# Weight scales from a norm instead of a maximum, unscaled relu values, and a second split of the weights

## The chip, the cores and the metric

The kernel runs on one core of a Trainium2 chip. The metric is the device time of one execution in microseconds; before the change the median of three runs is 1149.46 us.

## The reference

Attention with a mask that comes from clusters is followed by two expert layers. All of it is computed in float32:

```python
def _attn_ref(q, k, v, centroids):            # q, k, v (2, 8, 768, 64), centroids (8, 16, 64)
    q_n = q / (np.linalg.norm(q, axis=-1, keepdims=True) + 1e-06)      # k_n, c_n alike
    q_assign = np.argmax(np.einsum('bhsd,hcd->bhsc', q_n, c_n), axis=-1)
    mask = q_assign[:, :, :, None] == k_assign[:, :, None, :]
    scores = np.where(mask, scale * np.matmul(q, k.transpose(0, 1, 3, 2)), -1e9)
    attn = softmax(scores)
    return np.matmul(attn, v)

def _moe_ref(x, w_in, w_out):                 # x (1536, 512), w_in (512, 2048), w_out (2048, 512)
    h = x @ w_in
    return (h * np.clip(h + 3.0, 0.0, 6.0) / 6.0) @ w_out

def _moe2_ref(x, domain_probs, w1, w2):       # w1 (4, 512, 1024), w2 (4, 1024, 512)
    p = domain_probs / (domain_probs.sum(-1, keepdims=True) + 1e-09)
    for e in range(4):
        out += p[:, e:e + 1] * (np.maximum(x @ w1[e], 0.0) @ w2[e])
```

## The kernel before

Every float32 product of the expert layers is made of three float16 matmuls: each operand is split into a high half (its float16 rounding) and a low half (the rest), and high x high, high x low and low x high are summed in PSUM (mm3, lines 966 to 968). For float16 to hold the values, each weight matrix of 512 x 512 is first multiplied by a scale. The scale comes from the matrix's largest absolute value, and what it takes away is given back in later factors (kt, wu, pq). GSC and XSC are fixed powers of two in that bookkeeping.

The work falls into stages: attention of batch 0 (Attn.turned); Moe1, the first layer, of batch 0; Moe2, the second layer, of batch 0 together with attention of batch 1 (Attn.block); Moe1 of batch 1; Moe2 of batch 1. A batch has 768 tokens in two blocks of 384. Moe1 runs over four chunks of 512 hidden columns, Moe2 over eight; a chunk has two weight matrices ("i" and "o", or "1" and "2"), each of four tiles of 128 x 512. In batch 1 all chunks but the first use a scheme with seven instead of eight block products (class Wino, PSUM pool ps_w), which needs sums of weight blocks (sums_w).

Three helpers prepare weights. conv_w (line 936) takes the first layer's matrices, which arrive as float64 words, and builds float32 tiles from the bits (lines 947 to 955: an Abs on ScalarE, four VectorE instructions a tile, the first of which also accumulates the maximum). load_w (898) takes Moe2's matrices for batch 0: four raw tiles loaded (raw_w, 888), an absolute maximum of each on VectorE (903). Both then call allmax (510) to get one number for all 128 partitions. Without a PSUM pool it writes the column of maxima to DRAM (516), reads it back spread to all partitions (518) and takes a maximum over it (519). Then split_w (866) scales the tiles (GpSimd, for "2" ScalarE), rounds the high half (ScalarE, 874), subtracts the low half (GpSimd, 875) and writes the pair to DRAM as hl_* (886). again_w (908) reads these pairs; Moe1 reads them in both batches, Moe2 in batch 1. sums_w (915) loads the raw tiles of "1" once more for its sums.

Moe2.post (1199) turns a result of the first product into the operand of the second: Relu from PSUM with scale GSC into a float32 tile t (1202, ScalarE), the high half h[:, 0] from t (1203, ScalarE), and the low half h[:, 1] from t and h[:, 0] (1204, VectorE or GpSimd). A product's PSUM tile comes from p_m, three banks, in batch 0, and from ps_w, five banks, in the Wino chunks.

The order of instructions on every engine is fixed when the program is built: class Order takes all tasks with a priority (the table PAR and offsets in the code set it), places each on its engine at the time its own cost table says is earliest, lower priority numbers first, and emits them in that order. Each engine, SyncE's DMA queue too, then works its list strictly in order. Buffers come from pools in groups; the PSUM group of batch 0's attention (g_pa, with the pool ps_ma) closes before the group with p_m opens.

## Time and profile before

| | us |
|---|---|
| runs | 1149.46 median (1140.43 to 1151.48, three runs) |
| profiled execution | 1153.14 |
| its span, first to last instruction | 1151.4 |
| TensorE busy, instructions | 985.5 (86%), 5669 matmuls |
| VectorE busy | 792.5 (69%) |
| ScalarE busy | 566.8 (49%) |
| GpSimd busy | 398.9 (35%) |
| DMA, all 16 engines | 150.89 MB, mean 131 GB/s |
| mean granted TensorE clock | 0.938 of full speed |

PE is TensorE, PEld its weight loads, DVE VectorE, ACT ScalarE, POOL GpSimd, SP SyncE; a q behind a name is that engine's sequencer, so SPq is where SyncE's DMA instructions are issued and wait. In the table a busy share is a mean over stages with different limits, so the rows further down go by stretches. An instruction is named by its line in the listing above and by "out<-in" in the program's names.

### The profile page before, as it was taken

The page shows a single profiled execution, that of the slowest core. Times are in us where ns is not written, and L with a number is a line of the kernel's source. Part 1 is how long each engine was busy: PE and PEld are TensorE (multiplying, and loading weights), DVE is VectorE, ACT ScalarE, POOL GpSimd, SP SyncE. Part 2 cuts the span into 40 slices and gives each one's busy share as a digit, 9 for nine tenths or more (in the row PEclk, how much of TensorE's full clock was granted, in tenths as well). Part 3 has the DMA queues.
Part 4 walks back from the last instruction along what each step waited for, and adds up shares of the span by engine and source line. Part 5 has one row for each costly group of instructions (what it writes and reads, how often), then busy time and mean ns, then how long its engine had stood idle before and what let it go on. Part 6 is the DMA issues. An engine that isn't in the chain of part 4 may idle for free.

```text
span 1151.4 us, 16297 instructions
## 1 busy us (share of the span) xinstructions
PE 985.5 (86%) x5669; PEld 574.1 (50%) x5669; DVE 792.5 (69%) x1636; ACT 566.8 (49%) x1070; POOL 398.9 (35%) x376
## 2 busy tenths in 40 slices
...
GB/s 299 100 84 118 136 184 138 258 213 104 118 126 117 140 79 196 153 142 130 145 159 163 144 172 106 191 161 151 112 117 110 65 67 86 106 109 74 73 38 55
DMA packets 145778, 150.89 MB, mean 131 GB/s; under 512 B 86880, under 2 KB 89952, under 8 KB 145696
## 3 DMA queue, kind: packets, MB, share of 16 engines
...
## 4 chain that ended last, share of the span: by engine, by line
PE 44%; DVE 19%; DMA 18%; issue 9%; POOL 6%; ACT 3%; SPq 1%; POOLq 0%; ACTq 0%; DVEq 0%
DMA pt<-p 6%; PE psm L966 5%; PE psm L968 5%; PE psm L967 5%; PE psg L966 4%; PE psg L967 4%; PE psg L968 4%; PE psw L1043 4%; PE psw L1045 4%; PE psw L1044 4%; DVE ut L830 3%; DMA wraw<-in_w 3%; DVE p L854 2%; POOL w L875 2%; DMA bc<-mx 1%
## 5 line engine op out<-in xcount | busy, mean ns | idle before, releaser
L968 PE MATMUL psm<-w,h 128*128 128x512 f16 x384 | 149.6, 390 | 17.6 <-DVE h L1204 12.7
L966 PE MATMUL psm<-w,h 128*128 128x512 f16 x384 | 150.0, 391 | 0.0
L967 PE MATMUL psm<-w,h 128*128 128x512 f16 x384 | 149.3, 389 | 0.0
L1204 POOL TENSOR_TENSOR h<-t,h 128x384 f16<-128x384 f32 x32 | 29.2, 919 | 330.6 <-ACT h L1203 310.7
L831 ACT ACTIVATE e<-pss,ut 128x768 f32<-128x768 f32 x96 | 86.2, 899 | 90.5 <-DVE ut L830 54.1
L967 PEld LDWEIGHTS <-w 128*128 128x128 f16 x704 | 70.5, 100 | 66.0 <-issue 25.0
L966 PE MATMUL psm<-x2h,w 128*128 128x384 f16 x288 | 98.4, 342 | 1.9 <-ACT x2h L1161 1.4
L1204 DVE TENSOR_TENSOR h<-t,h 128x384 f16<-128x384 f32 x96 | 68.5, 714 | 45.6 <-ACT h L1203 45.4
L967 PE MATMUL psm<-x2l,w 128*128 128x384 f16 x288 | 97.9, 340 | 0.5 <-DVE x2l L1163 0.5
L966 PEld LDWEIGHTS <-w 128*128 128x128 f16 x704 | 70.5, 100 | 54.1 <-issue 12.3
L968 PE MATMUL psm<-x2h,w 128*128 128x384 f16 x288 | 97.4, 338 | 0.0
L968 PEld LDWEIGHTS <-w 128*128 128x128 f16 x704 | 70.7, 100 | 51.4 <-issue 8.1
L830 DVE TENSOR_REDUCE ut<-pss 128x1 f32<-128x768 f32 x96 | 90.3, 946 | 8.7 <-PE pss L825 8.3
L1229 DVE SCALAR_TENSOR_TENSOR oa<-psm,pq,oa 128x512 f32<-128x512 f32 x84 | 62.6, 745 | 46.5 <-PE psm L968 45.9
L875 POOL TENSOR_TENSOR w<-wraw,w 128x512 f16<-128x512 f32 x64 | 81.3, 1284 | 32.6 <-ACT w L874 27.6
L966 PE MATMUL psg<-g,w 128*128 128x384 f16 x256 | 84.1, 329 | 3.9 <-DVE t L1110 3.4
L967 PE MATMUL psg<-g,w 128*128 128x384 f16 x256 | 84.2, 329 | 0.9 <-POOL g L1112 0.6
L823 PE MATMUL pss<-ka,qa 128*128 128x384 f32 x192 | 64.1, 417 | 23.5 <-ACT e L831 21.4
L968 PE MATMUL psg<-g,w 128*128 128x384 f16 x256 | 84.1, 329 | 0.0
L739 PE MATMUL pst<-ident,e 128*128 128x128 f32 x288 | 49.3, 309 | 33.6 <-ACT pt L746 16.1
L903 DVE TENSOR_REDUCE am<-wraw 128x1 f32<-128x512 f32 x64 | 42.7, 677 | 50.3 <-DMA wraw<-in_w 50.2
L968 PEld LDWEIGHTS <-h 128*128 128x128 f16 x384 | 38.4, 100 | 69.2 <-DVE h L1204 22.6
(197 smaller groups left out, 2352.9 us busy)
## 6 DMA issues: line engine op xcount, KB each, us to landing
wraw<-in_w SPq DMA_DIRECT2D x92, 256.0 KB, 4.5
hl<-w SPq DMA_DIRECT2D x64, 256.0 KB, 4.3
w<-hl SPq DMA_DIRECT2D x64, 256.0 KB, 3.1
...
w<-hl_i SPq DMA_DIRECT2D x32, 256.0 KB, 3.6
w<-hl_o SPq DMA_DIRECT2D x32, 256.0 KB, 3.8
...
```

The source lines that it names most:

```text
L739: nc.tensor.transpose(ps[:, t // 3, t % 3 * 128:t % 3 * 128 + 128], e[:, x:x + 128], ident.t)
L823: nc.tensor.matmul(ps[:, f, 0:HS], qa[:, qs], ka[:, f * HS:f * HS + HS], start=True, stop=False)
L830: dve(S, p, lambda: nc.vector.tensor_reduce(out=nb(), in_=ps[:, :, 0:HS], axis=AX.XY, op=ALU.max, negate=True), [ps], [(tb, n)])
L831: act(S, p, lambda: nc.scalar.activation(out=e.t.rearrange("p (a b) -> p a b", a=2), in_=ps[:, :, 0:HS], func=AF.Exp, bias=nb(), scale=1.0 ...
L875: pool(512, p, lambda w=w, raw=raw: nc.gpsimd.tensor_tensor(out=w[:, 1], in0=raw.t, in1=w[:, 0], op=ALU.subtract), [raw, (w, 0)], [(w, 1)])
L966: nc.tensor.matmul(o_, ah, bh, start=i == 0, stop=False)
L967: nc.tensor.matmul(o_, ah, bl, start=False, stop=False)
L968: nc.tensor.matmul(o_, al, bh, start=False, stop=i == 3)
L1043: nc.tensor.matmul(o_, ah, bh, start=k == 0, stop=False)
L1044: nc.tensor.matmul(o_, ah, bl, start=False, stop=False)
L1204: low = lambda e: e.tensor_tensor(out=h[:, 1], in0=t.t, in1=h[:, 0], op=ALU.subtract)
L1229: dve(512, p, lambda: nc.vector.scalar_tensor_tensor(out=oa[:, t], in0=ps.t, scalar=q, in1=oa[:, t], op0=ALU.mult, op1=ALU.add), [ps, qk], ...
```

## The change

The scale of a weight matrix comes from its Frobenius norm. load_w squares each raw tile on ScalarE with an accumulated sum; conv_w squares the accumulated maxima of its tiles instead of reducing them. The new helper norm adds over partitions with a matmul against a tile of ones, sums four columns and clamps on VectorE, takes the square root as a power on GpSimd and the reciprocal on VectorE. The DRAM way of allmax is gone; its PSUM way stays for activations. conv_w is given a PSUM pool: ps_ma for the first two matrices, p_m for the other six.

Moe2.post rounds the relu straight from PSUM to the high half and gets the low half from PSUM too, always on VectorE; the tile t and the factor GSC are gone. Moe2's pairs are no longer written to DRAM in batch 0: in batch 1 the raw tiles are loaded and split again (split_w), and sums_w uses these tiles. The numbers of PAR are others, and Order adds 1.5 us (spm) to what a DMA waits for when it plans.

```diff
-XSC = 8192.0
-GSC = 2.0 ** -20
+XSC = 8.0
+WSC = 256.0
...
-    ta=43.32610950668564,
-    tu=2.3993615910477435,
+    ta=44.84286963635529,
+    tu=2.588310665078212,
...
-    mx=30.0,
-    sp=14.0,
-    spc=4.0,
+    mx=31.25809700336469,
+    sp=10.020641134361943,
+    spc=4.775375938290964,
...
-    slow=1.1868260418282515,
+    slow=1.0810926227241242,
...
-    cv0=90.0,
-    cvd=22.0,
+    cv0=130.0,
+    cvd=16.891660848559347,
+    cva=2,
...
-                                s = max(s, o.end)
+                                s = max(s, o.end + (PAR["spm"] if e == "SP" else 0.0))
...
-    ones = fixed([1, 128], F32, "ones")
+    ones = fixed([128, 128], F32, "ones")
...
+    def norm(am, cols, p, pp):
+
+        inv, ki, sc, ks = cols
+        ps = Buf(pp, [128, 4], F32, "psn")
+        pe(0.25, p, lambda: nc.tensor.matmul(ps.t, ones.t, am[:, 0:4], start=True, stop=True), [am], [ps])
+        dve(4, p, lambda: nc.vector.tensor_reduce(out=inv, in_=ps.t, axis=AX.X, op=ALU.add), [ps], [ki])
+        dve(1, p, lambda: nc.vector.tensor_scalar(out=inv, in0=inv, scalar1=1e-30, scalar2=1.0 / WSC ** 2, op0=ALU.max, op1=ALU.mult), [], [ki])
+        pool(2, p, lambda: nc.gpsimd.tensor_tensor(out=inv, in0=inv, in1=half[:, 0:1], op=ALU.pow), [], [ki], ns=172.0)
         dve(1, p, lambda: nc.vector.reciprocal(out=sc, in_=inv), [ki], [ks])
...
             if dst is None:
                 wt.setdefault(key, []).append(w)
+                continue
...
-            dma(262e3, p + (0 if dst else 4), lambda w=w, scr=scr: nc.sync.dma_start(out=scr.t, in_=w.t), [w], [scr])
+            dma(262e3, p, lambda w=w, scr=scr: nc.sync.dma_start(out=scr.t, in_=w.t), [w], [scr])
...
-            dve(512, p - PAR["mx"], lambda k=k, raw=raw: nc.vector.tensor_reduce(
-                out=am[:, k:k + 1], in_=raw.t, axis=AX.X, op=ALU.max, apply_absolute_value=True), [raw], [(am, k)])
-        allmax(am, 4, inv, ki, 1.0 / XSC, sc, ks, p - PAR["mx"])
+            act(512, p - PAR["mx"], lambda k=k, raw=raw: nc.scalar.activation(
+                out=mxj.t, in_=raw.t, func=AF.Square, accum_out=am[:, k:k + 1]), [raw], [(am, k)], acc=True)
+        norm(am, wcol(*key[1:]), p - PAR["mx"], p_m)
...
-                if key[1] == "1":
-                    act(512, p, lambda x=x: nc.scalar.activation(out=x.t, in_=x.t, func=AF.Copy, scale=sc), [ks], [x], ap=True)
...
-        allmax(am, 4, inv, ki, 1.0 / XSC, sc, ks, p, bits=True)
+        dve(4, p, lambda: nc.vector.tensor_tensor(out=am[:, 0:4], in0=am[:, 0:4], in1=am[:, 0:4], op=ALU.mult), [], [am])
+        norm(am, wcol(*key[1:]), p, pp)
...
-                again_w(key, p)
+                raws = raw_w(lambda k: src[:, k], p - 4)
+                split_w(key, raws, p)
                 if n == "1" and self.wino(c):
-                    sums_w(key, lambda k: src[:, k], p)
+                    sums_w(key, raws, p)
...
-            t = Buf(p_t[self.b], [128, MB], F32, "t")
             h = Buf(p_gw if self.wino(c) and blk else p_g, [128, 2, MB], F16, "h")
-            act(MB, p, lambda: nc.scalar.activation(out=t.t, in_=out(), func=AF.Relu, scale=GSC), [ps], [t], ps=True)
-            act(MB, p, lambda: nc.scalar.activation(out=h[:, 0], in_=t.t, func=AF.Copy), [t], [(h, 0)])
-            low = lambda e: e.tensor_tensor(out=h[:, 1], in0=t.t, in1=h[:, 0], op=ALU.subtract)
-            if PAR["hl"][self.b][f] == "P":
-                pool(MB, p, lambda: low(nc.gpsimd), [t, (h, 0)], [(h, 1)])
-            else:
-                dve(MB, p, lambda: low(nc.vector), [t, (h, 0)], [(h, 1)])
+            act(MB, p, lambda: nc.scalar.activation(out=h[:, 0], in_=out(), func=AF.Relu), [ps], [(h, 0)], ps=True)
+            dve(MB, p, lambda: nc.vector.scalar_tensor_tensor(
+                out=h[:, 1], in0=out(), scalar=0.0, in1=h[:, 0], op0=ALU.max, op1=ALU.subtract), [ps, (h, 0)], [(h, 1)])
...
-        conv_w((0, n, c), (w_in, w_out)[i % 2][c], G["cv0"] + G["cvd"] * i)
+        conv_w((0, n, c), (w_in, w_out)[i % 2][c], G["cv0"] + G["cvd"] * i, p_tn[i >= G["cva"]])
```

How this moves instructions stands in the program's order (of the rows an engine's list holds there, without times). First SyncE's DMA list in the second layer of batch 0, at the first transposes of batch 1's attention (pt<-p). Before, line 518 reads back a maximum, 788 are the transposes, 886 writes split pairs, 893 loads raw tiles:

```order
L562 DMA nat<-in_nat 128x768
L518 DMA bc<-mx_187 128x128
L788 DMA_TRANSPOSE pt<-p 128x12x128
L886 DMA hl_183<-w 128x1024
L893 DMA wraw<-in_w 128x512
L886 DMA hl_184<-w 128x1024
L893 DMA wraw<-in_w 128x512
```

After (783 are the transposes, 889 the raw loads, 557 loads attention's rows, 585 copies its queries):

```order
L889 DMA wraw<-in_w 128x512
L783 DMA_TRANSPOSE pt<-p 128x12x128 x2
L889 DMA wraw<-in_w 128x512 x2
L783 DMA_TRANSPOSE pt<-p 128x12x128
L889 DMA wraw<-in_w 128x512 x2
L783 DMA_TRANSPOSE pt<-p 128x12x128
L557 DMA nat<-in_nat 128x768
L783 DMA_TRANSPOSE pt<-p 128x12x128
L585 DMA qb<-qa 64x768
L783 DMA_TRANSPOSE pt<-p 128x12x128 x3
```

The writes of pairs and the two DMAs of each maximum have left the list; raw loads and transposes follow each other directly.

Second, VectorE's list at the end of batch 0's attention, around the last x1l (line 764, the low half of attention's output). Before, 948 to 954 convert tiles of the first layer, 1110 belongs to the first layer's own work, and 519 to 534 turn a maximum that came through DRAM into a scale:

```order
L952 SCALAR_TENSOR_TENSOR wconv<-r_2177,wconv 128x512
L954 SCALAR_TENSOR_TENSOR wconv<-r_2177,wconv 128x512
L948 TENSOR_SCALAR wconv,am<-wconv 128x512
L950 TENSOR_SCALAR wconv<-wconv 128x512
L512 TENSOR_REDUCE am<-am 128x1
L952 SCALAR_TENSOR_TENSOR wconv<-r_2248,wconv 128x512
L954 SCALAR_TENSOR_TENSOR wconv<-r_2248,wconv 128x512
L764 SCALAR_TENSOR_TENSOR x1l_783<-psv,vm,x1h_760 128x256
L1110 SCALAR_TENSOR_TENSOR t<-t,psg_2278 128x384
L519 TENSOR_REDUCE wv<-bc 128x1
L529 TENSOR_SCALAR wsc<-wv 128x1
L531 SCALAR_TENSOR_TENSOR wv<-wv,wsc 128x1
```

After (939 to 945 convert, 759 is the output's low half, 1105 belongs to the first layer, 947 to 951 square the accumulated maxima, 526 sums the result of the matmul with ones):

```order
L943 SCALAR_TENSOR_TENSOR wconv<-r_1929,wconv 128x512
L743 COPY pt<-pst 128x384
L1105 SCALAR_TENSOR_TENSOR t<-t,psg_1918 128x384
L945 SCALAR_TENSOR_TENSOR wconv<-r_1929,wconv 128x512
L947 TENSOR_SCALAR am<-am 128x4
L949 SCALAR_TENSOR_TENSOR am<-am 128x4
L951 TENSOR_TENSOR am<-am 128x4
L1105 SCALAR_TENSOR_TENSOR t<-t,psg_2055 128x384
L759 SCALAR_TENSOR_TENSOR x1l_690<-psv,vm,x1h_676 128x256
L1105 SCALAR_TENSOR_TENSOR t<-t,psg_2136 128x384
L1105 SCALAR_TENSOR_TENSOR t<-t,psg_2164 128x384
L526 TENSOR_REDUCE wv<-psn 128x1 x2
```

Ahead of the last x1l VectorE's list held the conversion of 24 of 32 tiles, and now holds 16; the other 16 follow it, in between the first layer's work. The first two norms that use the pool p_m stand right behind it.

Third, ScalarE's list at the first exps of batch 0 (831, now 826), where 573, now 568, takes the square roots of the row norms:

```order
L947 ACTIVATE wconv<-r_462 128x512
L573 ACTIVATE n_361<-n_361 128x72
L947 ACTIVATE wconv<-r_480 128x512
L947 ACTIVATE wconv<-r_493 128x512
L831 ACT_TABLE_LOAD
L831 ACTIVATE e,ut<-pss,ut 128x768 x3
L746 ACTIVATE pt<-pst 128x384
```

After:

```order
L558 ACTIVATE nat<-nat 128x768
L826 ACT_TABLE_LOAD
L826 ACTIVATE e,ut<-pss,ut 128x768
L568 ACT_TABLE_LOAD
L568 ACTIVATE n_270<-n_270 128x72
L938 ACTIVATE wconv<-r_403 128x512
L826 ACT_TABLE_LOAD
L826 ACTIVATE e,ut<-pss,ut 128x768
```

The square roots of the other pairs stood ahead of the first exp and now stand behind it, so the list holds two table loads more.

## Rows read from the trace of the kernel before

**Rows 1.** Five stretches: busy time (instructions) of each engine, TensorE clock, DMA share, GB/s.
```profile
0.00:200.00 200.00, 136.88 (x838) 99.42 (x839) 170.86 (x408) 133.75 (x261) 108.60 (x104) 0.89 0.58 152
200.00:345.00 145.00, 128.47 (x748) 75.00 (x747) 75.07 (x169) 63.47 (x114) 64.27 (x67) 0.94 0.64 163
345.00:785.00 440.00, 363.83 (x2096) 205.14 (x2094) 295.68 (x561) 207.87 (x385) 196.81 (x173) 0.91 0.73 149
785.00:905.00 120.00, 118.10 (x725) 70.63 (x723) 104.50 (x225) 62.66 (x115) 0.00 (x0) 1.00 0.32 107
905.00:1152.00 247.00, 238.18 (x1270) 123.92 (x1268) 146.41 (x278) 99.01 (x196) 29.22 (x32) 1.00 0.23 75
```

**Rows 2.** Chain of waits from 345 to 785 us, shares by line.
```profile
by line: DMA pt<-p 16.6%; issue 13.0%; DMA wraw<-in_w 8.1%; DVE p L854 5.5%; POOL w L875 4.3%; PE psm L966 4.3%; PE psm L968 4.2%; PE psm L967 4.1%; DVE ut L830 3.3%; PE psv L801 3.1%; DMA vr<-in_vd 2.9%; DVE h L1204 2.7%; DMA kb<-so 2.5%; 
```

**Rows 3.** The four passes of batch 1's attention, columns as in group 1: fourth pass first.
```profile
731.00:771.00 40.00, 39.95 (x265) 24.99 (x264) 30.05 (x56) 19.37 (x41) 13.29 (x13) 1.00 0.73 159
419.00:476.00 57.00, 44.43 (x260) 26.93 (x259) 41.62 (x79) 31.98 (x61) 33.03 (x29) 0.86 0.92 158
532.00:587.00 55.00, 42.52 (x250) 25.13 (x248) 41.83 (x70) 29.53 (x57) 30.37 (x27) 0.90 0.83 140
633.00:689.00 56.00, 44.52 (x268) 27.52 (x266) 41.07 (x76) 30.31 (x58) 30.77 (x27) 0.91 0.91 157
```

**Rows 4.** Line 903 (maxima of raw weights) alone, fourth pass: VectorE busy (instructions), clock, DMA, GB/s.
```profile
731.00:771.00 40.00, 0.00 (x0) 1.00 0.73 159
```

**Rows 5.** SyncE's waits, 345 to 785 us: total us, times, longest.
```profile
SPq L516 <- DVE am L512: 52.4, 8, 25.5
SPq L886 <- POOL w L875: 45.9, 20, 13.3
```

**Rows 6.** Groups, 345 to 785 us: count, busy us, mean ns, idle before.
```profile
L1204 DVE TENSOR_TENSOR h<-t,h 128x384 f16<-128x384 f32 x64 | 50.6, 793 | 19.5 <-ACT h L1203 19.2
...
L903 DVE TENSOR_REDUCE am<-wraw 128x1 f32<-128x512 f32 x56 | 37.3, 678 | 50.3 <-DMA wraw<-in_w 50.2
...
L1203 ACT ACTIVATE h<-t 128x384 f16<-128x384 f32 x64 | 33.4, 522 | 1.8
```

**Rows 7.** DMA issues, 345 to 785 us: count, KB, median us to landing.
```profile
hl<-w SPq DMA_DIRECT2D x56, 256.0 KB, 4.6
```

**Rows 8.** Lines 1204 (905 to 1152 us) and 1110: ns min/median/max, starts.
```profile
L1204 DVE TENSOR_TENSOR h<-t,h x32: 543/558/560, 907.3 to 1124.5; 128x384 f16<-128x384 f32 x32
...
L1110 DVE SCALAR_TENSOR_TENSOR t<-t,psg x40: 540/553/556, 199.7 to 808.7; 128x384 f32<-128x384 f32 x40
```

**Rows 9.** Groups of the whole span: conversion and split of the first layer's weights.
```profile
L875 POOL TENSOR_TENSOR w<-wconv,w 128x512 f16<-128x512 f32 x32 | 39.9, 1261 | 15.6 <-ACT w L874 15.6
...
L952 DVE SCALAR_TENSOR_TENSOR wconv<-r,wconv 128x512 int32<-128x512 int32 x32 | 28.0, 878 | 0.1
L954 DVE SCALAR_TENSOR_TENSOR wconv<-r,wconv 128x512 int32<-128x512 int32 x32 | 27.1, 850 | 0.2
...
L873 POOL TENSOR_SCALAR wconv<-wconv,wsc 128x512 f32<-128x512 f32 x32 | 25.0, 793 | 12.0 <-DVE wsc L534 11.9
...
L948 DVE TENSOR_SCALAR_CACHE_REDUCE wconv<-wconv 128x512 f32<-128x512 f32 x32 | 21.4, 672 | 20.9 <-ACT wconv L947 20.7
...
L950 DVE TENSOR_SCALAR wconv<-wconv 128x512 int32<-128x512 int32 x32 | 19.5, 613 | 0.3
```

**Rows 10.** Groups of the whole span: accumulator reads and a table load on ScalarE.
```profile
L831 ACT ACTIVATION_READ_ACCUMULATOR e<-pss,ut 128x1 f32 x96 | 18.9, 197 | 0.0
...
L831 ACT ACT_TABLE_LOAD x1 | 1.3, 1283 | 1.4 <-DVE n L638 1.4
```

**Rows 11.** DMA issues, 200 to 345 us.
```profile
hl_i<-w SPq DMA_DIRECT2D x8, 256.0 KB, 7.0
...
w<-hl_i SPq DMA_DIRECT2D x8, 256.0 KB, 5.9
```

**Rows 12.** SyncE's waits, 905 to 1152 us.
```profile
SPq L912 <- PE psm L968: 128.1, 25, 29.8
```

96 lines of the change are left out of this document (40 added, 56 removed).

## Prediction

> **What bounds the kernel now.** I read the stretches first [rows 1]. The program runs through five stages, and I call them A (attention of batch 0, to 200 us), B (first expert layer of batch 0, to 345), C (second layer of batch 0 together with attention of batch 1, to 785), D and E (first and second layer of batch 1). The reader is to see that D and E are TensorE's: it is busy 118.1 of 120 and 238.2 of 247 us at full clock, so nothing that other engines gain there is worth time. A is nearer VectorE's (170.9 of 200 us) than TensorE's (136.9). In B TensorE has 128.5 of 145. C is the longest, 440 us, and no engine fills it: TensorE 363.8 at a granted clock of 0.91, VectorE 295.7, a DMA share of 0.73.
>
> Why C takes that long stands in its chain of waits [rows 2]: the transposing DMA pt<-p is the largest share, 16.6%, then "issue" (13.0%), loads of raw weights (8.1%) and the VectorE and GpSimd steps around them. It runs in four passes, one for each head pair of batch 1. The stretches of the four [rows 3], from the first exp of a pair to its last, take 57, 55, 56 and 40 us, with twelve exps in each. In the first three, TensorE is busy for 44.4, 42.5 and 44.5 us at a clock of 0.86 to 0.91; in the fourth it is busy throughout at 1.00 (2.4 GHz; a mean below it means stretches at 1.2). The fourth is the one in which no weights are prepared (not one maximum over raw weights [rows 4], and so no split and no write to DRAM): GpSimd is busy 13.3 us there and 30 to 33 in the others, VectorE 30.1 and 41 to 42. So preparing weights costs about 16 us in each of three passes, 48 us in all, and that is the prize that C holds.
>
> **The change part by part.** *Maxima.* In C VectorE loses 56 maxima over raw weights at 678 ns, 37 us [rows 6]. ScalarE gets as many squares with an accumulator, a form that the trace doesn't have; by its copy of 384 elements at 522 ns [rows 6], scaled to 512 (696), and the accumulator's read of 197 [rows 10] one is about 0.89 us. The new order has 48 squares in C: 43 us, against 64 copies at 522 ns, 33 us, that the relu part takes from ScalarE. It ends 10 us heavier on 207.9 of 440, which leaves room.
>
> The way through DRAM goes too. SyncE's queue is served in order, and in C it stood 52.4 us in front of the write of the maxima and 45.9 in front of the hl writes that wait for GpSimd's split [rows 5], with transposes and loads queued behind. The 56 hl writes of 256 KB take 4.6 us each to land [rows 7]. All of these are gone from C, the hl writes and the two DMAs of each maximum, with 14.7 of the 65.5 MB that 149 GB/s move in 440 us [rows 1]. In their place stands a matmul, three VectorE instructions of a column and one power on GpSimd per matrix. VectorE's and GpSimd's part is a handover there and back, below 2 us by the sizes of such rows; it is hidden as long as the raw weights come early, and their tiles are written 32 to 46 us of TensorE work before the first use in C, where it was 7 to 38 (matmul columns counted in the order between the two, at the 163 ns that 384 of them take in D: 120 us for 725 matmuls [rows 1]).
>
> *Relu.* The second half h now reads the PSUM result instead of a copy. Before, h read two SBUF tensors and took 793 ns in C [rows 6] but 558 in E, where GpSimd is nearly idle [rows 8]; an instruction with the same shape of work and one PSUM operand took 540 to 556 ns in every stage [rows 8]. I take 553: 64 x 0.240 = 15 us less of VectorE in C. The Trainium skill (GPSIMD Engine Reference, section 1, Specifications) says that GpSimd shares its SBUF interfaces with VectorE and contends with VectorE instructions that have two SBUF inputs; the 793 against 558 agree, and by that rule the one-PSUM form escapes it, while a plain count of elements would give no gain here.
>
> So in C VectorE has 37 + 15 us less of 295.7, SyncE no longer stands in front of writes, and DMA carries a fifth less. What stays of the 48 us is the raw load and the split, in a pass eight GpSimd subtractions of 1.26 us and four scalings of 0.79 (13 us, by the like rows of the first layer [rows 9]). Bounds are 0, if the split alone makes the passes long, and 48. With the GpSimd half left and the VectorE, SyncE and DMA half gone I take half: **C -24**.
>
> *Conversion of the first layer's weights.* A tile costs VectorE 672 + 613 + 878 + 850 ns = 3.0 us [rows 9]. By the order 24 of the 32 tiles stood ahead of the last attention output of batch 0, now 16 do, because the norms from the third matrix on need a PSUM pool that opens only when attention closes its own. A loses 8 x 3.0 = 24 us of its 170.9 on VectorE, and 8 splits on GpSimd (16 us). At the same busy share of 85% it would end 28 us earlier; TensorE's 136.9 us, at a clock of 0.89 [rows 1], lies not far below what is then left, so I take half of that, **A -15**, between -28 and 0. Against it stand two further table loads on ScalarE, which the order shows between the first exps (square roots of the norms now come behind the first exp). One took 1.28 us [rows 10]: 2.6 us on an engine busy 133.8 of 200. The Trainium skill (ScalarE: Activation LUTs, section "What ACT_TABLE_LOAD costs") puts a switch at about 2.66 us with its drain; no run here shows the drain, and by that figure the two would be 5.3 us and A -12.
>
> B takes these 24 us on VectorE and 24 instead of 16 splits, while eight maxima leave; on GpSimd some splits of the second layer's first weights come forward too (16 us). VectorE comes to some 94 and GpSimd to about 97 of 145: none fills up. But the second pair of matrices is now normed when attention has closed, and by the order its reads back stand 6 to 13 us of TensorE work ahead of the first use (before: 34 to 37). A write of hl_i landed after 7.0 us and a read after 5.9 in B [rows 11], one waiting for the other. I charge **B +5**: bounds -5 (the waits for maxima through DRAM gone) and +30 (all six sets late by 5 us).
>
> *Second batch split anew.* E gains 64 x 1.261 + 32 x 0.793 = 106 us on GpSimd, idle there but for 29.2, and 32 x 0.553 = 18 us on VectorE (146.4 of 247). The loads have room: SyncE waited 128.1 us in E for TensorE to free a weight buffer [rows 12], and in the new order each split starts about 35 us of TensorE work before its first use. Cover is TensorE's own 238 us; without it the chain of four splits (8 us a matrix) would show 16 times. **D and E +1**, between 0 and +4.
>
> **Sum.** -15 + 5 - 24 + 1 = -33 against the profiled execution, 1153.1 us with its 1151.4 us span: 1120. The median of the runs is 1149.5, 3.7 lower, so 1117. With every bound at its end it is 1068 to 1183.
>
> **Rivals.** First, C doesn't move: the passes are held by transposes and GpSimd's splits, which stay. For it speaks the 16.6% of pt<-p in the chain, against it the fourth pass, which has the transposes and runs at 40 us. C then gives 4, and the time is 1137. Second, B is late: every set of converted weights holds TensorE for 5 us, +30 instead of +5: 1142. For it speak the short leads, against it that of the six sets only this pair's two have leads under 13 us. Third, slower than before: the PSUM bank of a relu is now freed by VectorE's h, not by ScalarE's first pass, and h stands in VectorE's order behind attention's instructions. Three banks serve C; one is filled by twelve matmuls at 163 ns, 1.96 us, so a bank may stay 3.9 us. ScalarE's pass (0.52 by its copy [rows 6]) and h take about 1.1, and 2.8 us of queue, three or four VectorE instructions of 0.7 to 0.8 us, stay free of charge. If more stands in front and each of the 64 tiles waits 0.75 us, C gets +48: 1165. It decides from 0.7 us a tile ((33 + 11.5) / 64). Against it: VectorE has 52 us less to do there.
>
> **How the numbers follow.** Chances: forecast 0.60 (its own range 1087 to 1133), C unmoved 0.17, B late 0.14, banks 0.09. The range 1087 to 1144 takes in the first three cases and leaves the last and the tails out. One per cent is 11.5 us, about what a measurement of this kernel can tell from no change: 1138 and 1161. Faster takes the forecast, most of the second case and a third of the third, 0.75; same 0.17; slower 0.08, which is nearly the fourth.
>
> **What would show it.** The three loaded passes near 48 us each with a clock above 0.91, SyncE's waits on the maxima and hl lines gone, h near 0.55 us: C right. The last attention output of batch 0 some 15 us earlier with VectorE's share still above 80%: A right. TensorE waiting at the reads of hl_i or hl_o at the start of B: the second rival. TensorE waiting for h in C again and again, right after h's own wait in VectorE's queue: the third. TensorE below full in E would prove the split anew not hidden.

## The result and the profile after

The changed kernel takes 1042.74 us (median of four runs, 1041.31 to 1044.12) against 1150.47 (1140.43 to 1151.55) for the kernel before: a ratio of 0.9081, 95% interval 0.9028 to 0.9134. That is 108 us, more than three times the 33 that I forecast, and below the whole range (1087 to 1144). The profiled execution has a span of 1040.9 us, TensorE at a mean granted clock of 0.986 (before 0.938) and 125.19 MB of DMA traffic (before 150.89).

For the comparison I cut both spans at the same events: A ends with the last attention output of batch 0 (psv<-pt,vr), B with the first product of its second layer (psm<-x2h,w), C with the last output of batch 1 (psv<-pt,vh). Rows of these tiles in the changed kernel (count, ns min/median/max, first and last start):

```profile
L750 PE MATMUL psv<-pt,vr x288: 378/379/635, 52.9 to 171.9; 128*64 128x256 f32 x144
...
L961 PE MATMUL psm<-x2h,w x288: 322/326/527, 314.9 to 828.2; 128*128 128x384 f16 x144
...
L796 PE MATMUL psv<-pt,vh x288: 269/273/422, 383.8 to 667.8; 128*64 128x256 f16 x144
```

By the same tiles the kernel before has 206.4, 351.1 and 782.9. The stretches, first of the kernel before (columns as in [rows 1]):

```profile
0.00:206.00 206.00, 142.85 (x872) 103.20 (x874) 176.69 (x420) 136.68 (x267) 109.52 (x105) 0.88 0.58 152
206.00:351.00 145.00, 127.89 (x749) 74.37 (x746) 73.54 (x165) 62.39 (x111) 64.31 (x67) 0.95 0.62 157
351.00:783.00 432.00, 356.44 (x2053) 201.00 (x2051) 289.99 (x549) 204.96 (x379) 195.86 (x172) 0.91 0.74 150
783.00:1152.00 369.00, 358.28 (x2004) 195.54 (x2001) 252.30 (x504) 162.72 (x313) 29.22 (x32) 1.00 0.26 87
```

And of the changed kernel:

```profile
0.00:172.00 172.00, 134.21 (x886) 97.29 (x886) 152.46 (x369) 129.75 (x255) 90.79 (x92) 0.99 0.44 138
172.00:315.00 143.00, 127.28 (x758) 74.47 (x755) 95.15 (x202) 79.29 (x153) 90.88 (x92) 0.98 0.57 193
315.00:668.00 353.00, 330.69 (x2076) 193.50 (x2073) 240.20 (x471) 204.94 (x416) 200.66 (x186) 0.99 0.59 138
668.00:1041.00 373.00, 361.85 (x2006) 196.66 (x2004) 272.08 (x539) 169.66 (x317) 104.12 (x96) 0.99 0.20 67
```

| stage | before | after | change | forecast |
|---|---|---|---|---|
| A | 206.4 | 171.9 | -34.5 | -15 |
| B | 144.7 | 143.0 | -1.7 | +5 |
| C | 431.8 | 352.9 | -78.9 | -24 |
| D and E | 368.5 | 373.1 | +4.6 | +1 |

C carries the miss. In it TensorE's idle time falls from 75.6 to 22.3 us, and its busy time from 356.4 to 330.7 at a clock of 0.99 for 0.91: of 79 us, 53 are waits that went and 26 the clock that came back as they went. To see where in C they lie, here are its parts in the changed kernel: lead-in to the first exp, then the four passes (from a head pair's first exp to its last) with the gaps between them:

```profile
315.00:361.80 46.80, 41.62 (x223) 22.21 (x221) 32.43 (x74) 28.96 (x57) 28.34 (x26) 0.93 0.52 168
361.80:408.20 46.40, 41.40 (x269) 25.31 (x268) 38.90 (x72) 33.82 (x70) 38.52 (x35) 1.00 0.75 155
408.20:447.00 38.80, 37.55 (x236) 20.93 (x234) 19.00 (x43) 20.47 (x43) 20.45 (x21) 1.00 0.41 113
447.00:492.60 45.60, 40.61 (x268) 25.01 (x265) 36.42 (x65) 32.04 (x68) 30.37 (x28) 1.00 0.72 142
492.60:532.60 40.00, 39.02 (x242) 21.33 (x243) 17.41 (x36) 19.88 (x42) 16.46 (x17) 1.00 0.35 97
532.60:577.80 45.20, 41.90 (x267) 26.53 (x266) 36.93 (x68) 31.92 (x67) 32.42 (x29) 0.96 0.75 144
577.80:617.80 40.00, 39.54 (x245) 21.85 (x244) 24.12 (x53) 15.26 (x28) 17.66 (x17) 1.00 0.38 100
617.80:656.80 39.00, 37.83 (x254) 23.90 (x253) 29.30 (x56) 16.14 (x33) 13.90 (x13) 1.00 0.70 149
```

And the lead-in and the three gaps of the kernel before, whose passes stand in [rows 3]:

```profile
351.00:418.40 67.40, 44.82 (x207) 21.93 (x205) 40.90 (x88) 21.90 (x36) 23.95 (x20) 0.82 0.64 118
475.70:531.00 55.30, 47.71 (x267) 24.93 (x265) 34.27 (x65) 25.29 (x46) 28.53 (x24) 0.93 0.67 164
587.00:632.80 45.80, 41.34 (x231) 21.23 (x230) 25.92 (x52) 18.57 (x35) 16.11 (x15) 0.90 0.65 156
689.00:730.70 41.70, 38.81 (x231) 21.50 (x230) 24.96 (x55) 19.51 (x37) 16.68 (x16) 0.96 0.49 134
```

The passes come to 46, 46, 45 and 39 us: I forecast "near 48", and they gave 33 of the 79. The other 46 lie outside them, nearly all in the lead-in (67.4 to 46.8) and the gaps (142.8 to 118.8), which my sum had left at nothing.

Waits in C (total us, times, longest), first TensorE's for transposes in the kernel before:

```profile
PE psv L801 <- DMA pt<-p: 26.1, 8, 7.2
```

And of the changed kernel:

```profile
SPq L889 <- POOL w L870: 63.0, 32, 19.9
...
ACT mxj L898 <- DMA wraw<-in_w: 13.6, 14, 4.5
...
PE psv L796 <- DMA pt<-p: 6.4, 7, 2.0
...
PE psm L963 <- DVE h L1197: 1.5, 2, 1.2
```

In the kernel before VectorE stood 50.2 us in front of maxima whose weights hadn't landed (the idle column of L903 in [rows 6]), and TensorE 26.1 us for transposes. In their place stand 13.6 us on ScalarE, in front of squares (L898), and 6.4 us. SyncE's wait for the maxima [rows 5] is gone. Its wait for GpSimd's split is not: it has moved from the hl writes (45.9 us) to the raw loads (63.0).

### The profile page after: what moved, and what is told of

It is laid out like the page before. It is cut to its first block, busy times and chain, and to the rows that moved or that the text cites. A ratio compares the mean times of both kernels' runs of the same rounds, so it can differ in the third digit from the quotient of the medians.

```text
span 1040.9 us, 16360 instructions
## 1 busy us (share of the span) xinstructions
PE 954.0 (92%) x5717; PEld 561.9 (54%) x5717; DVE 759.9 (73%) x1580; ACT 583.6 (56%) x1140; POOL 486.5 (47%) x464
## 2 busy tenths in 40 slices
DMA packets 125618, 125.19 MB, mean 120 GB/s; under 512 B 81568, under 2 KB 81568, under 8 KB 125536
## 4 chain that ended last, share of the span: by engine, by line
PE 41%; DVE 12%; DMA 5%; POOL 3%; ACT 3%; issue 1%; POOLq 0%; SPq 0%; DVEq 0%; ACTq 0%
PE psm L961 7%; PE psm L962 7%; PE psm L963 7%; PE psw L1039 4%; PE psw L1040 4%; PE psw L1038 4%; DMA pt<-p 4%; DVE p L849 2%; DMA wraw<-in_w 2%; PE psg L962 1%; PE psg L963 1%; PE psg L961 1%; POOL p L847 1%; PE psv L796 1%; ACT e L826 1%
## 5 line engine op out<-in xcount | busy, mean ns | idle before, releaser
L870 POOL TENSOR_TENSOR w<-wraw,w 128x512 f16<-128x512 f32 x128 | 155.7, 1239 | 164.2 <-ACT w L869 161.6
L963 PE MATMUL psm<-w,h 128*128 128x512 f16 x384 | 145.7, 380 | 2.7 <-DVE h L1197 2.7
L961 PE MATMUL psm<-w,h 128*128 128x512 f16 x384 | 146.0, 380 | 1.0 <-DVE oa L1219 0.9
L962 PE MATMUL psm<-w,h 128*128 128x512 f16 x384 | 145.7, 379 | 0.0
L961 PE MATMUL psm<-x2h,w 128*128 128x384 f16 x288 | 96.3, 334 | 7.9 <-DVE oa L1217 4.8
L963 PE MATMUL psm<-x2h,w 128*128 128x384 f16 x288 | 95.7, 332 | 0.0
L868 POOL TENSOR_SCALAR wraw<-wraw,wsc 128x512 f32<-128x512 f32 x64 | 52.7, 831 | 79.1 <-DMA wraw<-in_w 37.8
L869 ACT ACTIVATE w<-wraw 128x512 f16<-128x512 f32 x128 | 77.8, 625 | 19.5 <-POOL wraw L868 12.2
L818 PE MATMUL pss<-ka,qa 128*128 128x384 f32 x192 | 61.9, 404 | 16.0 <-ACT e L826 15.7
L1196 ACT ACTIVATE h<-psm 128x384 f16<-128x384 f32 x72 | 34.9, 484 | 61.6 <-PE psm L963 61.4
L722 POOL TENSOR_SCALAR e<-e,ut 128x768 f32<-128x768 f32 x48 | 45.8, 957 | 47.1 <-DVE ut L835 15.9
L1197 DVE SCALAR_TENSOR_TENSOR h<-psm,h 128x384 f16<-128x384 f32 x72 | 39.9, 554 | 36.8 <-ACT h L1196 36.3
```

Source lines behind the costliest of these rows:

```text
L722: sc = lambda eng, e=e, tb=tb: eng.tensor_scalar(out=e.t, in0=e.t, scalar1=tb[:, 2:3], scalar2=1.0, op0=ALU.mult, op1=ALU.mult)
L818: nc.tensor.matmul(ps[:, f, 0:HS], qa[:, qs], ka[:, f * HS:f * HS + HS], start=True, stop=False)
L868: pool(512, p, lambda raw=raw: nc.gpsimd.tensor_scalar(out=raw.t, in0=raw.t, scalar1=sc, scalar2=1.0, op0=ALU.mult, op1=ALU.mult), [ks], [ ...
L869: act(512, p, lambda w=w, raw=raw: nc.scalar.activation(out=w[:, 0], in_=raw.t, func=AF.Copy), [raw], [(w, 0)])
L870: pool(512, p, lambda w=w, raw=raw: nc.gpsimd.tensor_tensor(out=w[:, 1], in0=raw.t, in1=w[:, 0], op=ALU.subtract), [raw, (w, 0)], [(w, 1)])
L961: nc.tensor.matmul(o_, ah, bh, start=i == 0, stop=False)
```

## The experiments

All stage lengths are cut as above, in one profiled execution of each run. The kernel before spread from 1140 to 1166 us over its executions, and each set of runs had its own; so where a few us matter I go by the stage lengths.

| run | us | ratio (95%) | A | B | C | D, E |
|---|---|---|---|---|---|---|
| e1 new plan, old operations | 1125.4 | 0.9705 (0.9644 to 0.9765) | 203.0 | 145.4 | 403.7 | 370.2 |
| e2 old plan, new operations | 1072.8 | 0.9257 (0.9209 to 0.9304) | 189.0 | 148.6 | 361.3 | 370.9 |
| e3 changed, maxima on VectorE | 1048.8 | 0.9047 (0.9003 to 0.9092) | 172.9 | 143.5 | 359.3 | 373.5 |
| e4 before + norm, both layers | 1081.5 | 0.9330 (0.9285 to 0.9374) | 188.7 | 149.4 | 371.3 | 369.5 |
| e5 before + maxima by PSUM | 1093.7 | 0.9452 (0.9394 to 0.9510) | 208.6 | 137.3 | 377.6 | 368.4 |
| e6 before + squares, by DRAM | 1135.8 | 0.9800 (0.9720 to 0.9880) | 207.1 | 146.8 | 414.4 | 369.8 |
| e7 changed, total by DRAM | 1077.6 | 0.9320 (0.9264 to 0.9376) | 173.2 | 147.4 | 382.2 | 373.8 |
| e8 changed, conversion early | 1054.9 | 0.9132 (0.9075 to 0.9189) | 195.6 | 132.8 | 351.0 | 374.1 |
| e9 changed, old relu | 1058.5 | 0.9124 (0.9093 to 0.9154) | 173.8 | 144.2 | 360.5 | 380.0 |
| e10 changed, pairs by DRAM | 1047.3 | 0.9028 (0.9007 to 0.9050) | 172.5 | 144.2 | 359.8 | 367.6 |
| e11 before + split anew | 1149.1 | 0.9898 (0.9869 to 0.9927) | 207.5 | 144.6 | 418.6 | 377.6 |
| e12 changed, ten raw buffers | 1044.6 | 0.9006 (0.8986 to 0.9026) | 172.7 | 143.9 | 352.4 | 374.9 |
| e13 before, maxima on GpSimd's queue | 1161.5 | 1.0030 (1.0003 to 1.0058) | 208.1 | 140.0 | 446.0 | 369.8 |
| e14 the same on ScalarE's queue | 1170.9 | 1.0112 (1.0080 to 1.0145) | 208.1 | 146.2 | 446.2 | 369.2 |
| e15 before, write 12 us later in the plan | 1181.3 | 1.0190 (1.0143 to 1.0236) | 206.7 | 152.8 | 456.1 | 370.7 |
| e16 as e5, total 14 us later in the plan | 1109.4 | 0.9578 (0.9533 to 0.9622) | 206.9 | 143.0 | 389.9 | 369.5 |
| e17 as e5, total 28 us later in the plan | 1162.3 | 1.0043 (1.0016 to 1.0071) | 210.9 | 136.3 | 449.8 | 359.8 |
| e18 before + norm, second layer only | 1086.7 | 0.9376 (0.9320 to 0.9431) | 204.7 | 139.6 | 372.1 | 368.4 |

### Plan or operations: e1 and e2

e1 is the kernel before with the changed PAR and the DMA margin, e2 the changed kernel with the old ones:

```diff
-    mx=30.0,
+    mx=31.25809700336469,
...
-    cv0=90.0,
-    cvd=22.0,
+    cv0=130.0,
+    cvd=16.891660848559347,
...
-                                s = max(s, o.end)
+                                s = max(s, o.end + (PAR["spm"] if e == "SP" else 0.0))
```

> The kernel before with every operation as it was, but with the changed kernel's planner: its numbers of PAR (22 of them) and the 1.5 us that a DMA's start is put back in the plan. Theory P (the surplus over the forecast comes from the new numbers, which order the same work better): 1075 us or less, since 75 us of the 108 were not in my sum. Theory H (it comes from a queue's head: in the second layer of batch 0 VectorE stood 50 us in front of maxima for raw weights that hadn't landed, and SyncE 52 and 46 us in front of writes, with attention's instructions behind them; the numbers alone can't take these away): within 20 us of 1150, on either side.

> The changed kernel with all its operations, but with the numbers of PAR of before and without the 1.5 us of margin for DMAs (the pools for the first two norms stay the changed kernel's). Theory P: near my forecast, 1105 to 1125, as only the mechanisms are left. Theory H: 1045 to 1070, as the waits at the queue heads are gone with the operations, whatever the numbers.

e1 gave 33 us, 28 of them in C: too much for theory H, too little for P. e2 kept 86 of the gain and lies 3 us above what H allowed. The operations carry most of it; the numbers are worth about 29 us on top of them (span 1069.8 to 1040.9: A -17.1, B -5.6, C -8.4, D and E +2.2). My sum had no term for them.

### VectorE's work or the way through DRAM: e3 to e7 and e18

e3 puts the maxima of the changed kernel back on VectorE:

```diff
-            act(512, p - PAR["mx"], lambda k=k, raw=raw: nc.scalar.activation(
-                out=mxj.t, in_=raw.t, func=AF.Square, accum_out=am[:, k:k + 1]), [raw], [(am, k)], acc=True)
+            dve(512, p - PAR["mx"], lambda k=k, raw=raw: nc.vector.tensor_reduce(
+                out=am[:, k:k + 1], in_=raw.t, axis=AX.X, op=ALU.max, apply_absolute_value=True), [raw], [(am, k)])
...
```

> The changed kernel, but the second layer's raw weights are gone over on VectorE (an absolute maximum a tile, whose squares then go into the norm) and not squared on ScalarE; all else stays, so the weights' scale is another power of the data and the rest is as it was. By the price in my sum the 64 maxima of 0.68 us are some 37 us of VectorE time in a stage in which it is 68% busy, while ScalarE gets 43 us back: at most +10, 1043 to 1053. Theory H (what counts is what waits behind a maximum whose weights haven't landed): the maxima wait in VectorE's queue again and hold attention: +25 or more, 1068 to 1100, with VectorE's idle time in front of that line back above 25 us.

C grew by 6 us only, and VectorE's longest waits there were for TensorE and ScalarE (20.7 and 17.3 us); for raw weights it waited 3.4. Theory H falls as I put it: 37 us of maxima on VectorE are nearly free, as long as their weights are there. e4 adds norm, load_w's squares and conv_w's norm to the kernel before, and nothing else of the change:

> The kernel before with the norm alone: squares on ScalarE, the sum over partitions by a matmul with ones, no maxima on VectorE and none through DRAM, for both layers; relu, the hl writes and their reads, and the numbers of PAR stay as before. Theory H: at least 50 us faster, 1100 or less, as the two largest waits (VectorE for raw weights, SyncE for the maxima) go; the hl writes' 46 us of SyncE stay. By the forecast's sizes (a third to a half of the second layer's 24, the first layer's 15 only if its conversion moves): 1120 to 1135. Theory P: no faster than 1130, or slower, as the numbers were made for other operations.

It gave 77 us, 60 of them in C, without the relu, without the split anew, with the old numbers. So the surplus lies in the norm, and by e3 not in the move to ScalarE. That leaves the way of the total over the partitions. e5 changes it in one line, e6 changes the engine and keeps the way, e7 puts the way back into the changed kernel:

```diff
-        allmax(am, 4, inv, ki, 1.0 / XSC, sc, ks, p - PAR["mx"])
+        allmax(am, 4, inv, ki, 1.0 / XSC, sc, ks, p - PAR["mx"], pp=p_m)
```

> The kernel before with one edit: the largest value of a second-layer matrix goes over the partitions through PSUM (the transpose and the matmul with ones that the kernel has already for its activations), not through DRAM. The maxima stay on VectorE, all else stays. The norm on the kernel before gave 77 us in the last set of runs, and putting the maxima back on VectorE in the changed kernel took nothing away. Theory D (the way through DRAM was the cost: SyncE stands in front of the write until VectorE has the maximum, the raw loads stand behind it in the same queue, and VectorE stands in front of the next maximum until those loads land): 40 us or more faster than before, with VectorE's wait for raw weights, 50 us before, under 15. Theory V (VectorE's work on maxima is the cost, and the changed kernel's plan only hid it in the other run): within 15 us of before.

> The other half alone: the kernel before with the second layer's maxima replaced by squares on ScalarE, but the total still goes over the partitions through DRAM (a write, a broadcast read, a sum). Theory D: little, within 20 us of before, as SyncE still stands in front of each write. Theory V: 40 us or more faster, since VectorE has lost the 37 us of maxima and the 50 us of waiting for their weights.

> The changed kernel with one thing put back: the total of the second layer's squares goes over the partitions through DRAM, a write and a broadcast read of a matrix's sums, and not by a matmul with ones. Squares stay on ScalarE, and relu, split and plan stay changed. Theory D: 30 us or more slower than the changed kernel (ratio to before 0.935 or more), all of it in the second layer of batch 0, with SyncE's waits in front of the write back above 25 us. Theory V: within 12 us of the changed kernel (0.898 to 0.918).

e5: C is 54 us shorter by that one edit. VectorE's waits for raw weights in C of e5, then ScalarE's in C of e6:

```profile
DVE am L903 <- DMA wraw<-in_w: 9.2, 12, 1.6
```

```profile
ACT mxj L918 <- DMA wraw<-in_w: 33.0, 14, 5.9
```

In e6 the wait goes along to ScalarE, where exps and relus stand behind it, and C gets 17 of the 54. In e7 C is 29 us longer and the ratio 0.932, a little under the 0.935 I had asked for. SyncE's wait in front of the write is back there (31.9 us). So theory D holds in e5 and e6 (19 us faster, of the 20 it allowed) and misses its letter narrowly in e7: the way through DRAM is the cost. Whether it costs by SyncE's stand, as theory D had it, is the next question. e18 takes the norm for the second layer alone and completes the table of C: 432 (VectorE, DRAM), 414 (ScalarE, DRAM), 378 (VectorE, PSUM), 372 (ScalarE, PSUM).

> The kernel before with the norm for the second layer's weights alone: squares on ScalarE and the total through PSUM; the first layer's conversion, its maxima through DRAM and its place stay as before. It completes the table of the second layer of batch 0: VectorE and DRAM 432 us, ScalarE and DRAM 414, VectorE and PSUM 378, and here ScalarE and PSUM. If the two parts add up: 360 us. If the way through PSUM is nearly all of it, as the maxima on VectorE in the changed kernel cost only 6 us: 368 to 380. The first stage should end at 206 +- 3, as its 17 us come from the conversion's place.

It came to 372.1, as the second reading had it, with A at 204.7.

### What of the way through DRAM costs: e13 to e17

e13 and e14 leave the two DMAs of a second-layer matrix (those without bits) and take them out of SyncE's queue; e15 leaves them there and puts the write later. The write in e13:

```diff
-            dma(5e3, p, lambda: nc.sync.dma_start(out=dr.t.unsqueeze(1), in_=am[:, n:n + 1]), [(am, "r")], [dr], lag=G["ld"][0])
+            (add("POOL", 0.1, p, lambda: nc.gpsimd.dma_start(out=dr.t.unsqueeze(1), in_=am[:, n:n + 1]), [(am, "r")], [dr], lag=9.0) if not bits else dma(5e3, p, lambda: nc.sync.dma_start(out=dr.t.unsqueeze(1), in_=am[:, n:n + 1]), [(am, "r")], [dr], lag=G["ld"][0]))
...
```

> The kernel before with one edit: the write and the broadcast read of a second-layer matrix's maximum are issued from GpSimd's DMA queue, not from SyncE's. The way through DRAM, its latency, VectorE's maxima and all else stay; GpSimd now stands in front of the write instead of SyncE. Theory Q (what costs is the raw loads and transposes that stand behind the write in SyncE's queue): 30 us or more faster than before (ratio 0.974 or less), VectorE's wait for raw weights under 20 us, though GpSimd's own stand may take some back. Theory L (what costs is the round trip of two transfers, which makes every scale late, whoever issues them): within 15 us of before.

> As the run with GpSimd's queue, but the two DMAs of a maximum are issued from ScalarE's queue, with the exps and relus behind them. Theory Q: VectorE's wait for raw weights falls below 20 us here too, and the time lies between before and the run with GpSimd's queue, since ScalarE releases TensorE's banks and now stands in front of the write. Theory L: within 15 us of before, as the round trip is the same.

> The kernel before with the write of a second-layer maximum put 12 us later in the plan (it stays in SyncE's queue, and one to six raw loads that stood behind it now stand ahead of it). The round trip gets longer by that. Theory Q: 10 us or more faster than before, with SyncE's wait in front of the write under 30 us. Theory L: 10 us or more slower, as every scale comes later.

All three went against theory Q. GpSimd's and VectorE's waits in C of e13, then VectorE's in C of e15:

```profile
POOL mx L516 <- DVE am L512: 30.4, 4, 11.0
...
POOL bc L518 <- DMA mx<-am: 11.1, 4, 7.0
```

```profile
DVE am L903 <- DMA wraw<-in_w: 43.7, 25, 5.1
```

```profile
DVE am L903 <- DMA wraw<-in_w: 77.3, 26, 8.2
```

SyncE no longer stands in front of the write in any of them, and VectorE waits for raw weights nearly as long as before (43.7 us in e13, 45.7 in e14) or longer (77.3 in e15). (In e13 and e14 GpSimd and ScalarE stand instead, and SyncE stands longer in front of the hl writes, with raw loads behind them: 88.1 and 61.4 us, before 45.9. So these two alone don't clear the queue's head.) Landing of the write is no faster either: 8.5 us in the median in the kernel before, 9.2 in e13 and in e14, where 16 of the 24 writes come from the other queue. The Trainium skill (DMA: Bandwidth & Descriptors, section "Issuing engines are not separate DMA queues") says that DMAs of all issuing engines run on the same 16 DMA engines, so that another issuer saves only its sequencer's time; these landings agree.

Then the lateness without the DMAs: as e5, with a delay in the plan between a matrix's total and its transpose.

```diff
-        dve(n, p, lambda: nc.vector.tensor_reduce(out=am[:, n:n + 1], in_=am[:, 0:n], axis=AX.X, op=ALU.max), [am], [(am, "r")], lag=G["lr"])
+        dve(n, p, lambda: nc.vector.tensor_reduce(out=am[:, n:n + 1], in_=am[:, 0:n], axis=AX.X, op=ALU.max), [am], [(am, "r")], lag=late or G["lr"])
...
```

> The kernel before with second-layer maxima through PSUM (377.6 us for the second layer of batch 0, against 431.8), but the plan lets 14 us pass between a matrix's total and its transpose on TensorE, about what it lets pass for the two DMAs of the way through DRAM. So the scale is as late in the plan as before, with no DMA and nobody standing in front of one. Theory L (a late scale holds the eight buffers of raw weights, the next loads come late, and VectorE stands in front of the next maxima with attention behind it): most of the gain is given back, the second layer of batch 0 takes 410 us or more, and VectorE's wait for raw weights is 30 us or more. Theory Q (the two DMAs themselves, in whatever queue, with what stands behind them or shares the rings with them): the gain stays, 370 to 390 us, and that wait stays under 15.

> As the run with 14 us, with 28 us in the plan between the total and its transpose. Theory L: worse than with 14 us by 15 or more, near the late write in SyncE's queue (456 us for the second layer of batch 0). Theory Q: within 15 us of the run through PSUM without a delay, unless weights come too late for TensorE, which would show as TensorE waiting for the split.

By its letter e16 (389.9 us) is theory Q's. e17 (449.8) has theory L's time, but TensorE waits for the split there, 17.3 us in all and not at all in e5, and I had named that wait as what would leave theory Q standing. TensorE's waits in C of e17:

```profile
PE psm L966 <- ACT w L874: 7.9, 4, 3.7
PE psm L967 <- POOL w L875: 4.8, 6, 1.9
PE psm L968 <- POOL w L875: 4.6, 5, 1.3
```

Its loss lies elsewhere, too. Against e5 the lead-in and the gaps are longer (89 and 187 us for 57 and 120) and the four passes shorter (160 for 189), while in the kernel before the passes are long (210). So e17 shows that lateness with no DMA of a maximum can cost as much as the way through DRAM, but not that it costs in the same place.

The planned delay also says little of how late the scale really was. I took that from each trace: for the 14 matrices scaled in C, the time from the end of the fourth maximum or square to the end of the scale's reciprocal, and its mean.

| run | mean, us | C, us | wait for raw weights, us |
|---|---|---|---|
| e5 | 21.4 | 377.6 | 9.2 VectorE |
| e4 | 22.3 | 371.3 | 16.7 ScalarE |
| e18 | 22.4 | 372.1 | 17.4 ScalarE |
| e16 | 23.6 | 389.9 | 8.8 VectorE |
| e11 | 25.4 | 418.6 | 33.8 VectorE |
| e6 | 26.7 | 414.4 | 33.0 ScalarE |
| before | 28.1 | 431.8 | 50.2 VectorE |
| e13 | 29.8 | 446.0 | 43.7 VectorE |
| e14 | 29.9 | 446.2 | 45.7 VectorE |
| e17 | 34.7 | 449.8 | 31.5 VectorE |
| e15 | 38.8 | 456.1 | 77.3 VectorE |

The planned 14 us became 2 in e16, as TensorE's list took the transposes at other places anyway; 28 became 13 in e17. In the order of the real lateness C grows nearly without exception, whatever made the scale late, and in e16 and e17 no DMA of a maximum is in it. With the changed kernel's numbers e7 points the same way: 22.1 us and 352.9 in the changed kernel, 27.7 and 382.2 with the total through DRAM.

Three things keep this from being a proof. The order moves C, too: e1, with the old operations, is as late as the kernel before (28.3 us) and its C is 28 us shorter; and every edit makes the program plan all lists anew. In e12 the same mean is 27.2 us at a C of 352.4, because the squares end 4 us earlier and the scales come when they did. And there is no fixed price. The eight raw buffers hold two matrices, so 14 matrices, each holding its half 6.7 us longer (28.1 against 21.4), two at a time, come to 47 us (7 x 6.7), near the 54 of e5. By the same sum e15 should have added 75 us to the C of the kernel before and e17 46; they added 24 and 18.

One matrix of the kernel before shows what such a wait looks like. VectorE's list, then SyncE's, then all engines in the 10 us before and the 13 us between (columns of the last as in [rows 1]):

```profile
491.28 0.69 DVE L903 TENSOR_REDUCE am<-wraw 128x1 f32<-128x512 f32 x1 [0.61 <-DMA wraw<-in_w]
...
493.13 0.14 DVE L512 TENSOR_REDUCE am<-am 128x1 f32<-128x4 f32 x1
...
503.99 0.69 DVE L903 TENSOR_REDUCE am<-wraw 128x1 f32<-128x512 f32 x1 [8.02 <-DMA wraw<-in_w]
...
513.79 0.28 DVE L519 TENSOR_REDUCE wv<-bc 128x1 f32<-128x128 f32 x1
...
515.28 0.15 DVE L534 RECIPROCAL wsc<-wv 128x1 f32<-128x1 f32 x1
```

```profile
493.30 0.33 SPq L516 DMA_DIRECT2D mx<-am  x1
...
493.73 0.39 SPq L886 DMA_DIRECT2D hl<-w  x1
494.17 0.42 SPq L893 DMA_DIRECT2D wraw<-in_w  x1
...
504.61 0.33 SPq L518 DMA_DIRECT2D bc<-mx  x1
```

```profile
490.00:500.00 10.00, 8.52 (x73) 4.72 (x72) 5.35 (x8) 6.31 (x12) 10.00 (x9) 1.00 1.04 132
500.00:513.00 13.00, 9.47 (x38) 4.37 (x36) 7.08 (x14) 0.01 (x1) 0.19 (x1) 0.79 0.62 193
```

The reader is to see three things. The total is ready at 493.3 and the scale at 515.4, 22 us later, with two DMAs between. The raw load of 494.17 stood behind the write in SyncE's list; VectorE waits 8.02 us for the maximum that needs such a load, and all that is behind it waits too. From 500 to 513 ScalarE is busy for 0.01 us and GpSimd for 0.19, and TensorE's granted clock is 0.79 in the mean, after 1.00. The load itself took 9.8 us (494.17 to 503.99; the median in C is 5.0), with all DMA engines busy up to 500 (share 1.04), so their load may have a part in this wait. It doesn't explain C as a whole: in e11 raw loads land after 4.4 us in the median, as in e5, and C is 418.6.

### The other parts: e8 to e12

e8 puts the conversion of the first layer's weights back (23.5 of 32 tiles ahead of batch 0's last attention output, not 16):

```diff
-    cv0=130.0,
-    cvd=16.891660848559347,
-    cva=2,
+    cv0=90.0,
+    cvd=22.0,
+    cva=6,
```

> The changed kernel with the first layer's weight conversion where it stood before: the numbers that place it are those of before, and the first six norms (not two) take the PSUM bank that attention has, so that 23.5 of 32 tiles are converted ahead of batch 0's last attention output, not 16. All else stays. My sum said 15 us for this move, and the stage ended 34 us earlier; with the changed kernel's operations and the old numbers, also at 16 tiles, it ended 17 us earlier. If the conversion sets the end of that stage: the last output comes 20 to 35 us later than the changed kernel's 171.9, the next layer gives some 5 back, and the time is 1058 to 1075. If other numbers of the plan made the rest: only 10 to 17 later, 1048 to 1056.

The time is in the second reading's range and the stage in the first's. A ended 23.7 us later, so the conversion's place is most of A's gain; but B gave 10.2 back, twice what I took, and the sum is 12 to 13 us.

e9 puts the relu through a float32 tile again (the factor is 1):

```diff
-            act(MB, p, lambda: nc.scalar.activation(out=h[:, 0], in_=out(), func=AF.Relu), [ps], [(h, 0)], ps=True)
+            act(MB, p, lambda: nc.scalar.activation(out=t.t, in_=out(), func=AF.Relu, scale=1.0), [ps], [t], ps=True)
+            act(MB, p, lambda: nc.scalar.activation(out=h[:, 0], in_=t.t, func=AF.Copy), [t], [(h, 0)])
...
```

> The changed kernel with the relu of before: Relu from PSUM into a float32 tile t on ScalarE, the high half from t on ScalarE, the low half from two SBUF tiles on VectorE (GpSimd takes every second one in batch 1). No factor is needed, so the relu's scale is 1. All else stays changed. My sum took h from 793 to 553 ns, 15 us of VectorE in the second layer of batch 0, and named as a rival that h now holds the PSUM banks. If the relu's part is an ordinary small gain: 3 to 12 us slower than the changed kernel (ratio to before 0.911 to 0.919), with h from two SBUF tiles at 700 ns or more while GpSimd is busy. If h holding the banks costs something: same or faster than the changed kernel. If time in SBUF form is only elements over rate: h at 553 here too.

h in C, first of the changed kernel, then of e9 (count, busy us, mean ns, idle before):

```profile
L1197 DVE SCALAR_TENSOR_TENSOR h<-psm,h 128x384 f16<-128x384 f32 x64 | 35.4, 553 | 27.7 <-ACT h L1196 27.2
```

```profile
L1200 DVE TENSOR_TENSOR h<-t,h 128x384 f16<-128x384 f32 x64 | 44.0, 689 | 36.2 <-ACT h L1199 35.8
```

The ratio is in the range of an ordinary small gain, but the span is 17.6 us longer, where I had said 12 at most: C grew by 7.6 us and D and E by 6.9. The latter I hadn't seen. My reading, which no run tests, is that in batch 1 the old relu gives GpSimd 32 of the subtractions, and GpSimd now has the second split to do.

e10 writes the pairs of the second layer in batch 0 and reads them back (again_w), e11 splits anew on the kernel before (no hl writes; raw_w and split_w in batch 1):

```diff
-                raws = raw_w(lambda k: src[:, k], p - 4)
-                split_w(key, raws, p)
+                again_w(key, p)
...
```

> The changed kernel with the second layer's pairs written to DRAM in batch 0 and read back in batch 1 (only the raw weights for the sums are loaded and scaled again there), as before the change; all else stays changed. My sum counted the 46 us that SyncE stood in front of those writes, with transposes queued behind, as part of the second layer's gain. If that wait held attention: 12 us or more slower (ratio 0.918 or more). If it only stands elsewhere now (SyncE waits 63 us for the same GpSimd splits in front of the raw loads in the changed kernel): within 8 us of the changed kernel (0.901 to 0.915).

> The kernel before with this part alone: no pairs of the second layer are written to DRAM, and batch 1 loads and splits its weights again; maxima on VectorE and through DRAM, relu and plan as before. If SyncE's wait in front of the writes is a cost of its own: 15 us or more faster (ratio 0.987 or less). If SyncE's wait for the maxima rules as long as it is there, or the wait moves to the raw loads: within 12 us of before. Batch 1 itself should give 0 to 4 us away, as in the forecast.

e10: C +6.9, D and E -5.5, so this part as a whole is worth next to nothing. e11: C -13.2, D and E +9.1 (I had said 0 to 4), 10 us faster in the median, as the second reading had it: SyncE still stands 48.0 us in front of the maxima, and its wait for the split has moved to the raw loads.

e12 adds raw buffers:

```diff
-    p_wr = Pool("wr", 8, g_w)
+    p_wr = Pool("wr", 10, g_w)
```

> The changed kernel with ten buffers for raw weights, not eight. SyncE stands 63 us in front of raw loads in the second layer of batch 0 until GpSimd's split frees a buffer, with transposes behind it. If that wait is the next head of a queue that costs: 6 us or more faster than the changed kernel (ratio below 0.903). If the transposes behind it are not late (TensorE waited 6.4 us for them in all): within 5 us of it.

By the ratio it seems a gain, but its own time is 1044.6 against 1042.7 and C is 352.4 against 352.9: the kernel before was slower in that set. SyncE still waits 64.5 us in front of the raw loads, and it costs nothing. No run's own time is below the changed kernel's, which wasn't timed again beside them.

## Why the prediction was wrong

The direction, the stages and most mechanisms were right; one term was far too small, and one was missing. From the spans of before (1151.4), e18 (1084.8), e4 (1078.9), e2 (1069.8) and after (1040.9) the parts are: norm of the second layer -66.6, norm of the first -5.9, relu and split anew -9.1, numbers and margin of the plan -28.9.

**C, -24, measured -78.9.** The step that failed is "that is the prize that C holds", and the half of 48 after it: the norm of the second layer alone gave 59.7 us of C (e18). I took the fourth pass as what a pass costs without weights, and so bounded C's gain by the three loaded passes. But the weights' loop runs from the start of C to the last split, through the lead-in and the gaps as well, and 46 of the 79 us came from there; no bound may be taken from half of a stage. Then I priced the maxima by what they do (37 us of VectorE) and gave the way through DRAM no price of its own. e3 and e6 show that the first is small by itself (6 and 17 us of C), e5 that the second is 54. A sign of it stood in a column of [rows 6] that I printed and didn't use: 50.2 us of VectorE's idle time in front of L903, until a raw load landed. I should have asked why that load was late, and followed it back: to a split, to a scale, to a total on its way through DRAM. I even costed the new way (a matmul and a handover) and the old one as DMAs on a busy queue, but never put the two times from total to scale beside each other.

**The plan's numbers, 0, measured -28.9.** I took them for what moves the rows shown, and looked at the order in three places. Even on the old operations they gave 33 us (e1).

**A, -15, measured -34.5.** The mechanism was right: with the conversion's norm on the old numbers (e4 against e18) A gives 16.0, at 16 tiles ahead of the last output as I counted. Another 17.1 come with the new numbers (e2 to after). The two further table loads of 1.28 us stand there as I said. ScalarE's next instruction starts 0.02 us behind such a load (32.33 + 1.28, then 33.63), so no drain is added that this trace shows.

**B, +5, measured -1.7.** The charge was right in kind and too low: +9.8 by e4 against e18, 10.2 by e8; the second layer's norm took 5.1 off B (e18) and the plan's numbers 5.6 (e2 to after).

**D and E, +1, measured +4.6, just above my bound of 4.** 3.4 us of it lie in D, which I had given nothing: GpSimd's splits begin there (27.8 us of work where there was none). TensorE's idle time in D grows by 1.2 us and its busy time by 1.8, at a clock of 0.99 for 1.00. In e10, without those splits, D takes 124.9 us, as in the kernel before.

**Relu.** 553 ns, as I took it. e9 also shows the price of two SBUF inputs again: the same instruction takes 689 ns in C and 583 after it. The Trainium skill (GPSIMD Engine Reference, section 1, Specifications) has VectorE instructions with two SBUF inputs contend with GpSimd; these two numbers, with GpSimd busy for 57% and 35% of the stretch, agree. Taken one by one in the kernel before, the 54 that overlap no GpSimd instruction take 560 ns at most, and the 42 that do take 772 in the median and up to 1995.

**SyncE.** "SyncE no longer stands in front of writes" was half right. The wait for maxima is gone; that for the split moved to the raw loads and is longer (63.0 us), and hurts no one. Nor is it the length of SyncE's stand that C pays for: in e5 it stands 84.3 us in front of the hl writes, not much less than the 98.3 of both lines before, with C 54 us shorter.

**The rivals.** None came. TensorE waited 1.7 us for h in C, so the banks are no issue, and the reads of converted weights held nothing at the start of B. I had three ways to be too optimistic and none to be too pessimistic by more than 50 us; with every bound at its end my sum was 1068.

**What stays open.** That the total's way through DRAM costs 54 us of C is shown (e5), and that it costs in the changed kernel too (e7). By what it costs is not. That a late scale holds the eight buffers fits the waits and one sum of 47 us, fails by that sum in e15 and e17, and was not tried on the kernel before with more buffers. The share of SyncE's stand, in front of the write or of the hl writes behind a late split, isn't parted from that of the round trip, and the 17 us that the numbers give in A were not divided among them.
